# Ten value loads among the other loads, four-quadrant products, 4 KB output runs and hand-placed PSUM slots in a fused attention and token-mixing kernel

## The chip, the cores and the metric

One core of a Trainium2 chip. The metric is the device time of one execution in microseconds (us); most kernels ran 4 to 20 times, always beside the kernel before on the same chip. An execution counts as slow when it is over 1.5% above the fastest of its kernel; verdicts use the fast ones. A profile's span is about 2 us shorter than the time of its execution. Engines: PE is TensorE's products, PEld its weight loads, DVE is VectorE, ACT is ScalarE, POOL is GpSimd, SP issues the DMAs.

## The reference

Eight batches, eight heads, 576 tokens, head size 64. Attention in two parts, then a token-mixing MLP on x (576 x 512 per batch):

```python
q_d, k_d, v_d = (t.reshape(B, H, S // 4, 4, D).mean(axis=3) for t in (q, k, v))
out_up    = np.repeat(sm_attn(q_d, k_d, v_d), 4, axis=2)        # coarse
out_local = softmax(where(abs(i - j) < 4, q @ k.T / 8, -1e9)) @ v  # local band
x   = (out_up + out_local), heads side by side
w   = (x @ w_q) @ (x @ w_k).T / 8                                # per batch
out = maximum(w @ x, 0) @ w_out
```

## The kernel before

All loads and stores go through one DMA queue, issued by SP in program order. Per batch it loads q and k (1 MB each, runs of 1 KB), their last 64 tokens (`r`, runs of 256 B), and the value as ten pieces of 64 partitions (runs of 256 B):

```python
    def load_qk(b):
        q32 = big.tile([128, H, 4 * D], FP32, name="q32", tag="q32")   # two buffers each
        k32 = big.tile([128, H, 4 * D], FP32, name="k32", tag="k32")
        ...
        for src, t in ((q[b], q32), (k[b], k32)):
            sp.dma_start(t, _ap(src, 0, [[4 * D, 128], [S * D, H], [1, 4 * D]]))
        ...                                                             # r32 right behind
    def load_v(b):
        for n in range(NW):
            for c in range(2):
                sp.dma_start(v32[64 * c:64 * c + 64, n], ...)
```

The steps of several batches are interleaved by one list (the number is the batch relative to the iteration); a store is issued in the step that makes its rows:

```python
    ORDER = [
        (-2, "og1"), (-1, "wtd"), (0, "sums"), (1, "cast_qk"), (-1, "wt"), (0, "vd"), (0, "mask0"),
        (0, "score0"), (-1, "wks"), (2, "load_qk"), (1, "cast_v"), ...
        (2, "load_v"), (-1, "og0"), (0, "ca1"), (1, "tk"), (1, "tr"), (-1, "ol"), (0, "xt0"), ...
    ]
    def og(i):
        ...
        evac("og%d" % i, os_, p_)                                       # ACT, three buffers os
        sp.dma_start(out[b, 256 * i:256 * i + 256].rearrange("(m p) d -> p m d", p=128), os_)
```

Names used below, in the order of a batch: `psc` masks and local scores, `pcs` coarse scores, `pv` pooled value, `pav` local attention times value, `pca` coarse attention times value, `pw` and `pws`/`pwk` the projections, `pm` the product that `M` comes from, `pmx` the mixed rows (`rmx` after the relu), `po` and `pol` the last product.

The softmax here doesn't subtract the row's maximum and nothing guards it: scores larger than these inputs give would overflow.

## Time and profile before

| | before |
|---|---|
| time, median of 3 runs | 192.36 us (191.82 to 193.6) |
| one batch, start of `pw` to start of the next | 19.30 us |
| PE busy of these | 18.52 us |
| last value load landed | 151.5 us |
| clock granted to PE, mean | 0.95 |

### The profile page before, as it was taken

Reading aid. Unit: us, or ns where it says so; the run is one execution under the profiler, and the core shown is the slowest. Engines: PE = TensorE matmul, PEld = TensorE weight load, DVE = VectorE, ACT = ScalarE, POOL = GpSimd, SP = SyncE. Lnnn points to the kernel's source line nnn. Section 1 sums busy time; section 2 is a strip of 40 time slices with the busy share of each in tenths; the row PEclk is TensorE's granted clock in tenths of the full one; section 3 lists DMA queues with packets and bytes.
Section 4 is the critical chain, followed back from the end, with each engine's and each line's share of the span. In section 5 each row is a group of like instructions: output and inputs, shape, how many; then the busy total and the mean of one; then the engine's idle time right before and its main releaser. Section 6 shows DMA issues by size and latency. Waiting matters only on the chain.

```text
span 192.7 us, 6374 instructions
## 1 busy us (share of the span) xinstructions
PE 155.5 (81%) x2720; PEld 104.0 (54%) x2720; DVE 114.8 (60%) x286; ACT 110.7 (57%) x140; POOL 107.7 (56%) x122
## 2 busy tenths in 40 slices
PE   0034448885899989998999899989998999898790
PEld 0034227853576647664776476647764776465330
DVE  6263978754646566656665666566656665685220
ACT  2037134954565767576757675767576757633422
POOL 5701991099748991895479547954895476000000
PEclk9999555999789999999999999999999999999997
DMA  5999999899899799967999899969996943004215
GB/s 175 314 187 215 348 290 162 191 354 175 175 319 218 174 264 294 263 137 201 278 323 156 184 280 346 187 154 296 330 215 154 300 146 112 3 3 153 93 57 188
DMA packets 74027, 40.54 MB, mean 210 GB/s; under 512 B 52432, under 2 KB 68880, under 8 KB 74000
## 3 DMA queue, kind: packets, MB, share of 16 engines
q1 hardware_dynamic: 73920, 40.12, 81.7%
q8 instruction: 21, 0.34, 0.7%
q14 instruction: 6, 0.05, 0.1%
q10 hardware_dynamic: 80, 0.03, 0.1%
HBM read 30.67 MB, written 9.44 MB: 208 GB/s over the span
## 4 chain that ended last, share of the span: by engine, by line
PE 68%; DVE 17%; ACT 7%; issue 4%; POOL 2%; ACTq 0%; DVEq 0%
PE po L27 15%; PE psc L27 6%; PE pav L27 5%; PE pw L27 4%; PE px L27 4%; PE pca L27 4%; PE pol L27 4%; DVE kd_127 L27 3%; PE pv L27 2%; PE pcs L27 2%; ACT kT L27 2%; PE pod L27 2%; DVE rz L27 1%; PE pws L27 1%; PE pwd L27 1%
## 5 line engine op out<-in xcount | busy, mean ns | idle before, releaser
L27 ACT COPY os<-po 128x1024 f32<-128x1024 f32 x16 | 16.2, 1012 | 14.7 <-issue 8.3
L27 DVE RECIPROCAL rz<-pav 128x8 f32<-128x8 f32 x40 | 8.1, 204 | 13.4 <-PE pav L27 13.4
L27 PE MATMUL po<-wo_91,rmx_227 128*128 128x512 f16 x64 | 15.3, 379 | 0.6 <-ACT rmx_227 L27 0.6
L27 PE MATMUL po<-wo_91,rmx_212 128*128 128x512 f16 x64 | 15.1, 379 | 0.0
L27 DVE COPY xT<-px 128x928 f16<-128x928 f16 (+1 forms) x32 | 13.8, 451 | 0.6
L27 PE MATMUL pq_236<-id_67,q_229 128*128 128x128 f16 x16 | 1.9, 312 | 12.6 <-DVE q_229 L27 12.6
L27 PE MATMUL psc<-id_67,neg 64*128 64x232 f16 (+1 forms) x80 | 9.4, 278 | 2.8 <-DVE vblk_201 L27 2.8
L27 PEld LDWEIGHTS <-rmx_227 128*128 128x128 f16 x80 | 7.2, 98 | 8.1 <-ACT rmx_227 L27 0.7
L27 PE MATMUL psc<-qT,kT 64*64 64x58 f16 (+1 forms) x640 | 11.4, 198 | 0.0
L27 PEld LDWEIGHTS <-rmx_212 128*128 128x128 f16 x80 | 7.2, 98 | 6.6
L27 DVE RECIPROCAL rc<-pca 128x8 f32<-128x8 f32 (+1 forms) x16 | 3.4, 211 | 11.8 <-PE pca L27 11.8
L27 PEld LDWEIGHTS <-wqk_90 128*128 128x128 f16 x96 | 8.3, 98 | 3.7 <-issue 0.9
L27 PEld LDWEIGHTS <-kT 64*64 64x64 f16 x640 | 8.7, 113 | 2.1 <-issue 2.1
L27 ACT COPY odT<-pod 128x448 f16<-128x448 f16 (+1 forms) x16 | 5.6, 402 | 6.3 <-PE pod L27 6.3
L27 PE MATMUL pw<-xT,wqk_90 128*128 128x288 f16 x64 | 9.2, 286 | 0.0
L27 PEld LDWEIGHTS <-q_229 128*128 128x128 f16 x16 | 1.6, 146 | 12.6 <-DVE q_229 L27 12.6
L27 POOL CAST v_0_147<-v_79 128x2560 f16<-128x2560 f32 x1 | 3.1, 3129 | 9.3 <-DMA w_92<-in_moe_w_k_dram 9.3
L27 DVE TENSOR_TENSOR wT_219<-pw,wTd 128x576 f16<-128x576 f32 x4 | 3.0, 758 | 8.6 <-ACT wTd L27 8.6
L27 DVE COPY ol<-pol 64x512 f32<-64x512 f32 x8 | 5.5, 682 | 4.3 <-PE pol L27 4.3
L27 DVE TENSOR_TENSOR wT_204<-pw,wTd 128x576 f16<-128x576 f32 x4 | 3.0, 758 | 8.0 <-ACT wTd L27 6.6
L27 DVE TENSOR_SCALAR rmx_227<-pmx 128x1024 f16<-128x1024 f32 x4 | 4.9, 1224 | 4.1 <-PE pmx L27 4.1
L27 POOL CAST v_1_149<-v_255 128x2560 f16<-128x2560 f32 x1 | 2.3, 2323 | 8.6 <-DMA v_255<-in_v_dram 8.6
(542 smaller groups left out, 540.9 us busy)
## 6 DMA issues: line engine op xcount, KB each, us to landing
out_dram<-os SPq DMA_DIRECT2D x16, 512.0 KB, 4.4
v_79<-in_v_dram SPq DMA_DIRECT2D x10, 128.0 KB, 4.6
v_255<-in_v_dram SPq DMA_DIRECT2D x10, 128.0 KB, 5.4
v_583<-in_v_dram SPq DMA_DIRECT2D x10, 128.0 KB, 3.5
v_1024<-in_v_dram SPq DMA_DIRECT2D x10, 128.0 KB, 4.4
v_1497<-in_v_dram SPq DMA_DIRECT2D x10, 128.0 KB, 3.6
v_1970<-in_v_dram SPq DMA_DIRECT2D x10, 128.0 KB, 4.3
v_2443<-in_v_dram SPq DMA_DIRECT2D x10, 128.0 KB, 3.4
```

The source lines that it names most:

```text
L27: return lambda *a, **k: self._tc.keep_in_program_order(f_(*a, **k))
```

## The change

Its intent: shorten TensorE's work (four tiles at once in `pav`, two column tiles at once in `pm`, one `pol` for two batches), relieve POOL and DVE, start earlier, write longer runs, and spread the ten slow value loads between the fast loads of q and k. The core of the diff:

```diff
-    ps2 = ctx.enter_context(tc.tile_pool(name="ps2", bufs=3, ...))
-    ps1 = ctx.enter_context(tc.tile_pool(name="ps1", bufs=2, ...))
+    free = {2: [0, 1, 2], 1: [3, 4]}          # a slot is taken when it is free, can be held
...
-    def load_qk(b): ...                       # q32, k32: 2 + 2 buffers
+    def load_q(i): ...                        # q or k; tag="in32", bufs=3 for both
+    def load_r(b): ...
+    def load_v(n): ...                        # one of five pairs of pieces
...
-            pool.tensor_copy(v16[:, :, :, 0:64], v32)
+            evac("va" ..., v16[:, :, 0:4, 0:64], v32[:, :, 0:4])                    # POOL
+            for c in range(2):                                                       # ACT, DVE
+                evac("vb%d" % c ..., v16[64 - 64 * c:128 - 64 * c, :, 4:8, 0:64],
+                     v32[64 * c:64 * c + 64, :, 4:8])
...
-                                tile_position=(64 * c, 64 * c))                      # pav
+                                tile_position=(o, 64 * c))                           # o = 64 * (c ^ s_)
...
-            evac("M2", M2[0:64], p_[0:64], scale=s_mix)
+                pe.matmul(p_[64 * c:64 * c + 64], w_, x_, ..., tile_position=(0, 64 * c))
+            act.copy(half, p_[64:128])
+            dve.tensor_tensor(M2[0:64], p_[0:64], half, op=ALU.add)
...
-                        pe.matmul(p_[:, ff, :], rmx[:, r * S + c:r * S + c + 128], ...)
-                sp.dma_start(out[...].rearrange("(m p) d -> p m d", p=128), os_)
+                        pe.matmul(p_[:, ff, :], _ap(rmx, 512 * r + 2 * i + ff, [..., [4, 128]]), ...)
+        def so(i):                             # the store is a step of its own, placed by ORDER
+            return lambda: sp.dma_start(_ap(out[b], 2 * i * DM, [[4 * DM, 128], [1, 2 * DM]]), ...)
...
+    FIRST = [ ... ]                            # the start and batches 0 to 4 by hand
+    ORDER = [
+        (3, "load_r"), (0, "wtd"), (0, "wt"), (-1, "og1"), (1, "vd"), (1, "mask0"), ...
+        (2, "cast_r"), (2, "load_k"), (1, "score1"), ... (2, "load_v0"), ... (3, "load_v2"), ...
+        (2, "load_v3"), (2, "load_v1"), ... (-2, "so1"), (0, "ol"), ... (-1, "sol"),
+        (2, "load_v4"), ... (0, "og0"), ... (3, "load_q"), (2, "cast_v"), (-1, "so0"), (2, "tk"),
+    ]
```

In the last lines, q and k of a batch are no longer next to each other in the queue; both stores of a batch are issued about a period after their rows are made; and q and k share three buffers. The cast of `r` goes from POOL to ACT.

## The prediction

> **What bounds the kernel now.** I read the page first (busy times, the 40 slices, the queues), then the chain that ended last, then a table of windows cut at the end of each batch's `pwd`, then the issues on the DMA queue in order of time. The chain says that TensorE sets the end; in its steady part one batch takes 19.30 us (start of `pw` to start of the next `pw`), on the chain almost only PE pieces:
>
> ```profile
> 81.83 0.98 PE pw L27 x8
> ...
> 85.46 0.37 PE pav L27 x16
> 85.83 1.62 PE pm_1793 L27 x7
> ...
> 96.72 0.86 PE pol L27 x4
> ...
> 101.13 0.98 PE pw L27 x8
> ```
>
> The windows agree: PE is busy 18.52 of 19.30 us, at the full clock. The columns behind the length are PE, weight loads, DVE, ACT, POOL, then clock, DMA share, GB/s:
>
> ```profile
> 81.83:101.13 19.30, 18.52 (x342) 12.43 (x341) 12.32 (x29) 13.17 (x18) 13.58 (x13) 1.00 0.87 235
> 159.03:176.31 17.28, 16.50 (x306) 10.41 (x305) 11.73 (x27) 9.49 (x16) 3.25 (x6) 1.00 0.20 71
> 176.31:192.70 16.39, 9.21 (x62) 4.06 (x59) 3.18 (x5) 5.20 (x8) 0.00 (x0) 0.93 0.29 104
> ```
>
> But there is a second limit nearly as tight. The page's slices show the DMA engines at nine tenths or more until three quarters of the run, and the queue's issues form one unbroken stream up to 150 us:
>
> ```profile
> DMA  5999999899899799967999899969996943004215
> GB/s 175 314 187 215 348 290 162 191 354 175 175 319 218 174 264 294 263 137 201 278 323 156 184 280 346 187 154 296 330 215 154 300 146 112 3 3 153 93 57 188
> DMA packets 74027, 40.54 MB, mean 210 GB/s; under 512 B 52432, under 2 KB 68880, under 8 KB 74000
> ...
> 88.94 0.57 SPq L27 DMA_DIRECT2D out_dram<-os  x1
> ...
> 98.62 10.27 SPq L27 DMA_DIRECT2D v_1970<-in_v_dram  x10
> 108.99 1.13 SPq L27 DMA_DIRECT2D out_dram<-os  x1
> ...
> 129.28 0.57 SPq L27 DMA_DIRECT2D out_dram<-os  x1
> ```
>
> From store to store this stream takes 20.05 and 20.29 us, longer than PE's 19.30. The rate swings between about 150 GB/s (value loads, packets of 256 B) and 350 (q and k, 1 KB). PE is not starved only because the loads start two batches ahead. The lead shrinks, and the last value load is the proof:
>
> ```profile
> 151.85 2.32 POOL L27 CAST v_1_149<-v_2916 128x2560 f16<-128x2560 f32 x1 [4.56 <-DMA v_2916<-in_v_dram]
> 159.94 0.40 PE L27 MATMUL pv<-v_1_149,P_153 128*32 128x512 f16 x1
> ```
>
> The last batch's value lands at 151.8, its cast ends at 154.2, its first product starts at 159.94. Only 5.8 us of slack are left, however fast the engines become.
>
> Third, the start. In the chain, DVE's `sum`, `kd` and `kdt` hold everything from 18.22 to 27.2 us, and q waits behind constant fills on DVE until 11.4.
>
> **What the Trainium skill says.** "TensorEngine Tiling (Array Packing)", section Tiling Modes, Key Properties: different tiles can run at once, and changing the tiling mode drains the engine. The trace agrees on the first: scores, which use four 64x64 tiles, start 32 products in 0.26 us, eight ns apart; `pav`, which uses two tiles, starts 16 in 0.25, sixteen apart. After the four 32-column `pv` products the next mode starts 0.33 us later, against 0.215 between full products of that width. "DMA: Bandwidth & Descriptors", section Why small descriptors are slow, says a 256 B descriptor pays a fixed overhead of about a quarter; here value loads do run at under half of q's rate, so the trace agrees in direction, with more loss. The same page, Specifications, gives line rate from 512 B up: for the stores, 2 KB already, it promises nothing for 4 KB. "GPSIMD Engine Reference", Specifications, says its SBUF interface is shared with VectorE when VectorE has two SBUF inputs; the trace fits: `kd` took 1487 ns on DVE for batch 0 (POOL was casting) and 383 on POOL later.
>
> **The change, part by part, per batch.**
> - `pav`: four tiles in turn, and the value of the upper heads lies in the other half. From sixteen to eight ns a product: 16 x 8 ns = 0.13 us x 5 = -0.65 us of PE.
> - `pm`: 7 full products of 0.216 us become column-tiled pairs, four rounds: -0.65 us, and about 0.1 back for mode changes. But the sum of the two halves now takes an ACT copy of 64x512 (0.59, as `M` had) and a DVE add (0.69, as `x`) in series: some 0.7 us longer on the path in the tail, where nothing hides it.
> - `pol`: the last 64 rows of two batches share one product: -0.86 in every second batch, -0.43 on average.
> - masks and `vd` are split (9 more products a batch, same columns): +0.15.
> - In the chain, 87.84 to 89.79 is PE waiting in turn for DVE to empty `pav`, because the slots rotate. A new order with slots taken as they come free may win half: -0.7 (estimate).
> - Sum -2.2: PE's period becomes about 17.1 us.
> - ACT gets the second `rmx` (1.02), half of the upper value cast (64x1280 at the k cast's 1898 ns per 2048: 1.2), the remainder cast (0.6) and copies (0.7), `half` (0.6), half of `ol` (0.3), and gives up `vd`, `wTd`, `wd`, `M`, `mxr` (2.1): 13.2 + 2.3 = 15.5 us. DVE goes 12.3 to about 12.8, POOL 13.6 to about 11.5. All fit below 17.
> - Stores: `os` in 128 runs of 4 KB instead of 256 of 2 KB. The weights of the product are then read at a stride of four; `pws` already loads such strided weights at under 40 ns a product, and `po` has 216 ns to hide it. Worth nothing by itself, perhaps 0.2 us a batch of DMA.
> - Start: k and q come in halves, k first; sums of batch 0 move to PE (36 products) and ACT; constants are filled later. `pav` of batch 0 needs the value, which cannot land before about 18.5 us with the same stream, so its 28.3 becomes about 21: -7 us.
>
> **If PE alone decided:** `pw` of batch 0 at 40.0 - 7 = 33; next at +21 (22.5 before) = 54; five periods of 17.1 and a last one 2 us shorter (it has no next batch's transposes, as before: 17.28 against 19.30) = 154.6; tail 16.4 + 0.7 for `half` + 1 for both `rmx` now in series on ACT - 0.7 (`pm`) = 17.4. End: 172 us.
>
> **If the loads decide.** The bytes in front of the last load stay: 30.67 MB read, and in both programs eight `os` and four `ol` stores stand before it on the queue. So the landing stays near 151.8, less what a better mixture gives. Value loads are the stretch at low rate; ten of them placed between q, k and stores may run while large packets drain. I give it 4 us (estimate; half a us a batch of the 20). Landing 148; cast in three parallel parts, 1.3: 149.3. From `pv` of the last batch to the end took 192.7 - 159.94 = 32.8; less the PE savings of that stage and the tail (0.65 + 0.55 x 2 + 0.7 for the waits, 0.4 for `pol`), plus 1.7 in the tail: 31.6, and without the waits of a full engine, say 30. End: 179 to 181.
>
> The larger one rules, but the mixture may give more than 4 us, so I choose **178 us**.
>
> **The rivals.**
> 1. PE period rules (172). For it: PE is 96% busy, and the loads get spread on purpose. Against it: 20.05 us of queue time per batch that no part of the change takes away.
> 2. Loads rule fully, mixture gives nothing: 183 to 185. For it: all packets remain 256 B. Against: half-idle slices (6, 6, 4) show that the value stretches do not fill the engines.
> 3. Less prefetch starves PE: q and k now share three buffers where they had four, and a value is loaded, cast and used within about an iteration less than before; ACT at 15.5 with waits between could also become the pace: 186 to 191. For: stores wait for ACT, casts for loads, loads for casts. Against: casts of the batch before always precede the loads that need their buffer in program order by half an iteration.
> 4. Column tiles do not overlap in `pm` or `pav`: +1.3 a batch on PE, 18.4, still below the queue's 20. It would cost little.
>
> **Range and chances.** 172 is the floor that PE sets, 185 is rival 2: I take 171 to 186 for eight in ten. 2% faster means below 188.5, which only rival 3 in full would miss: faster 0.93, same 0.06, slower 0.01.
>
> **What would show it.** Right: the wait before the last cast of `v` still on DMA, landing at 146 to 150, and `pv` of the last batch within 2 us of that cast; PE pieces separated by waits on casts of q, k or v in the steady part; period 17.5 to 19; DMA share at nine tenths to the end of loading; `pm` four rounds at about 0.9 us, `pav` 16 at about 0.15; first `pav` near 21. Wrong: if the last load lands before 143, the queue was not at its limit and rival 1 holds; if ACT is busy over 95% in the steady windows, or queue issues wait on POOL casts for long, rival 3 does; if value stretches run over 200 GB/s, the mixture was worth more than I gave it.

## More of the kernel before

The chain, the windows, the DMA slices and the issues are shown in the prediction. Two more rows of the page matter later: busy tenths of PE and the granted clock, in 40 slices of 4.8 us.

```profile
PE   0034448885899989998999899989998999898790
...
PEclk9999555999789999999999999999999999999997
```

After the start PE is full and its clock stays full.

## The result, and the profile after

The changed kernel took **198.25 us** (median of 4: 197.92 to 201.45, the last one slow), beside 192.77 for the kernel before in the same rounds. The ratio is 1.028, 95% interval 1.021 to 1.035: slower by nearly 3%. A ratio here is the mean time of one kernel's fast runs over that of the other's fast runs of the same rounds, so it is not quite the ratio of the medians quoted.

The same two rows of the page, and the DMA row:

```profile
PE   0639495788799399995998998699895999999690
...
PEclk9999858599999859998899999969997999999997
DMA  5999998999879999989599889997799972202225
```

PE now has holes in the middle of the run (the 3, 5, 6, 5), and the clock falls after each of them. The DMA engines are full to the end of loading, as before. Cut at each start of `pw` (columns as in the prediction: length, PE, weight loads, DVE, ACT, POOL, clock, DMA share, GB/s):

```profile
59.51:81.03 21.52, 18.01 (x348) 12.62 (x346) 12.72 (x32) 14.05 (x19) 13.82 (x10) 0.84 1.08 242
...
101.38:120.98 19.60, 17.92 (x352) 12.14 (x350) 13.47 (x33) 15.13 (x20) 9.24 (x8) 1.00 0.95 238
120.98:142.46 21.48, 18.46 (x348) 12.63 (x346) 12.50 (x31) 14.77 (x19) 11.76 (x8) 0.92 0.91 218
...
163.59:179.23 15.64, 14.86 (x312) 9.87 (x310) 13.23 (x31) 11.35 (x14) 4.50 (x4) 1.00 0.15 58
179.23:196.00 16.77, 10.47 (x72) 5.00 (x69) 3.35 (x9) 6.04 (x7) 0.00 (x0) 0.93 0.36 138
```

The five steady periods take 20.8 us on average, where 17.1 were predicted, and no engine is full in them. What PE waits for has several names. The first kind is a pause inside one group of products, with nothing to wait for (the bracket is the idle time before, and its cause):

```profile
64.80 0.25 PE L27 MATMUL psc_1434<-qT,kT 64*64 64x56 f16 x7
...
68.46 0.32 PE L27 MATMUL psc_1434<-qT,kT 64*64 64x56 f16 x9 [3.42 <-issue]
```

In the middle of sixteen equal products TensorE stands still for 3.4 us. The trace's DMA records have one 16,384 B packet of the instruction queue at 65.4 us that took 1.4; there are 22 such packets, and PE with its weight loads has 5,624 instructions, about 256 to a packet. I read this as TensorE waiting for its own next instructions, a fetch; experiment 2 tests it. The second kind is a store:

```profile
126.03 1.01 ACT L27 COPY os<-po_2675 128x1024 f32<-128x1024 f32 x1 [2.46 <-DMA out_dram<-os]
...
127.10 0.38 PE L27 MATMUL psc_2749<-id_64,neg 64*128 64x232 f16 x4 [1.51 <-ACT os L27]
```

ACT cannot empty `po` into an output buffer whose last store has not landed, and PE waits for the slot of `po`. The page of waits counts (total us, times, longest):

```profile
ACT os L27 <- DMA out_dram<-os: 9.2, 5, 2.9
...
PE psc_1434 L27 <- issue: 3.4, 1, 3.4
```

Two smaller pauses, 0.49 at 119 and 0.89 at 140 us before `pk`, are of the second kind too. Between 60 and 160 us half clock set in within 3.3 us of the beginning of each pause of 1.5 us or more:

```profile
67.30:74.20 6.90, 5.74 (x91) 3.59 (x91) 2.83 (x8) 4.20 (x7) 1.89 (x1) 0.51 0.97 263
74.20:91.20 17.00, 14.94 (x293) 10.51 (x292) 11.42 (x25) 13.26 (x17) 11.58 (x8) 1.00 1.06 243
91.20:94.70 3.50, 3.35 (x52) 1.82 (x55) 2.17 (x5) 1.46 (x2) 0.00 (x0) 0.51 0.66 116
```

The Trainium skill, "TensorE: Matmul & The Clock Gate", Part 1, gives the idle state half the clock and a window of about 3.4 us after which a busy array is granted the full one. The trace agrees with the length: the half-clock stretches last 3.4 or 6.8 us. It does not agree that a whole idle window is needed: a pause of 1.51 us at 125.6 was followed by half clock from 128.8 to 132.2. Counted over all 20 traces, the clock changes lie on a grid of 3.41 us. Of the 711 grid windows at full clock after 45 us, half clock followed all 40 in which PE stood idle for 45% or more, 4 of the 22 between 36 and 45%, and none of the 649 below. So it is the idle share of a grid window that counts, and not the length of one pause: the 1.51 us and another 0.46 lie in one window and leave it idle for 57%. Between 60 and 160 us there are 17.1 us at half clock here (none before), which cost PE up to half of that.

The end, with first and last start in us:

```profile
L27 PE MATMUL pv<-v_1_100,P4rep x2: 276/281/286, 166.7 to 166.9; 128*128 128x256 f16 x2
L27 POOL CAST v_1_100<-v_2855 x1: 1262/1262/1262, 158.8 to 158.8; 128x1280 f16<-128x1280 f32 x1
L27 ACT CAST v_1_100<-v_2855 x1: 1263/1263/1263, 162.8 to 162.8; 64x1280 f16<-64x1280 f32 x1
L27 DVE CAST v_1_100<-v_2855 x1: 1886/1886/1886, 163.6 to 163.6; 64x1280 f16<-64x1280 f32 x1
```

The last value landed at 158.1 (151.5 before; 148 predicted), its three casts ended at 165.5, the first `pv` began at 166.4, and the program ended 29.6 us later. "Landed" is here and below the end of the last load packet; what waits for it sees it 0.2 to 0.8 us later. Did PE wait for this value?

```profile
149.10:184.00 34.90, 33.74 (x627) 22.55 (x626) 25.05 (x60) 24.12 (x31) 13.74 (x11) 0.95 0.46 131
```

```profile
166.39 0.29 PE L27 MATMUL pv<-v_1_100,P_102 128*32 128x256 f16 x1
```

It did not. PE was busy for 33.74 of the 34.90 us around the landing, and no idle time stands in a bracket behind its first `pv`.

What became slower is on the DMA engines. Both kernels load the same 66,560 packets: 16,384 of 1 KB and 50,176 of 256 B. Summed over the trace's records and divided by 16 engines, they take **124.1 us before and 136.5 us after**: a 1 KB packet 52.1 and 58.0 ns, a 256 B packet 22.6 and 24.6. The stores became cheaper, 31.8 and 27.9 us. I call the first number the load time of a kernel; it is the measure that the experiments follow. It has two weaknesses. The packets' records overlap (the DMA share of the period from 59.51 above is 1.08), so a longer record is not as much more work. And each kernel has one profile: kernels that differ only in small products of PE differ by 0.6 to 3.0 us (after_fix and after_stream_so with and without `pad64` in the table below).

### The profile page after: what moved, and what is told of

Its sections match the earlier page's. It is cut to its first block, busy times and chain, and to the rows that moved or that the text cites.

```text
span 196.0 us, 6577 instructions
## 1 busy us (share of the span) xinstructions
PE 156.8 (80%) x2812; PEld 107.5 (55%) x2812; DVE 114.8 (59%) x300; ACT 129.2 (66%) x160; POOL 94.0 (48%) x112
## 5 line engine op out<-in xcount | busy, mean ns | idle before, releaser
L27 PEld LDWEIGHTS <-kT 64*64 64x64 f16 x640 | 8.0, 119 | 7.3 <-issue 5.7
L27 PEld LDWEIGHTS <-rmx_98 128*128 128x128 f16 x64 | 7.0, 114 | 5.6 <-ACT rmx_98 L27 0.4
L27 PEld LDWEIGHTS <-rmx_86 128*128 128x128 f16 x64 | 6.9, 113 | 5.0
L27 PEld LDWEIGHTS <-neg 64*128 64x128 f16 x112 | 4.3, 99 | 9.8 <-issue 9.4
L27 PEld LDWEIGHTS <-wqk_69 128*128 128x128 f16 x96 | 8.0, 98 | 2.1 <-issue 0.6
L27 PEld LDWEIGHTS <-k_163 128*128 128x128 f16 x32 | 3.3, 144 | 6.4 <-ACT k_163 L27 6.4
L27 PE MATMUL pk_173<-id_64,k_163 128*128 128x128 f16 x8 | 1.0, 310 | 5.7 <-POOL P_106 L27 5.7
L27 POOL CAST v_0_99<-v_2373 128x1280 f16<-128x1280 f32 x1 | 1.7, 1707 | 7.6 <-DMA v_2373<-in_v_dram 7.6
L27 POOL CAST k_2096<-k_1801 128x2048 f16<-128x2048 f32 x1 | 1.9, 1898 | 6.2 <-PE pav_2026 L27 6.2
L27 POOL CAST q_917<-q_856 128x2048 f16<-128x2048 f32 x1 | 1.9, 1890 | 6.1 <-DMA q_856<-in_q_dram 6.1
L27 DVE TENSOR_SCALAR wk_95<-pwk,rows 128x256 f16<-128x256 f16 (+1 forms) x8 | 2.0, 296 | 4.6 <-PE pwk L27 4.6
L27 POOL CAST v_2_101<-v_1898 128x1280 f16<-128x1280 f32 x1 | 1.7, 1701 | 6.2 <-DMA v_1898<-in_v_dram 6.2
L27 DVE CAST vd_0_80<-pv 128x512 f16<-128x512 f32 x4 | 2.8, 693 | 3.2 <-PE pv L27 3.2
L27 PEld LDWEIGHTS <-q_169 128*128 128x128 f16 x32 | 3.2, 141 | 2.5 <-DVE one_109 L27 1.4
L27 DVE CAST vd_1_92<-pv 128x512 f16<-128x512 f32 x4 | 2.8, 694 | 3.0 <-PE pv L27 2.8
L27 PE MATMUL pol<-wo_70,rest 128*128 128x512 f16 x16 | 4.4, 399 | 0.1
L27 ACT COPY qT<-pr 128x256 f16<-128x256 f16 x8 | 2.9, 368 | 2.1 <-PE pr L27 2.1
L27 POOL CAST k_1625<-k_1225 128x2048 f16<-128x2048 f32 x1 | 1.9, 1897 | 5.1 <-DMA k_1225<-in_k_dram 5.1
L27 PEld LDWEIGHTS <-M_0_84 128*128 128x128 f16 x32 | 2.5, 109 | 3.0 <-issue 1.4
L27 POOL CAST q_538<-q_509 128x2048 f16<-128x2048 f32 x1 | 1.9, 1895 | 4.6 <-DMA q_509<-in_q_dram 4.6
```

The costliest lines, as they stand in the source:

```text
L27: return lambda *a, **k: self._tc.keep_in_program_order(f_(*a, **k))
```

## The experiments

All runs together. "Load time" is the sum just described; a star marks a profile that fell on a slow run, so that its two numbers on the right are only indications.

| run | median us (runs) | ratio of fast runs to before | load time | last value landed |
|---|---|---|---|---|
| before | 192.77 (4) | 1 | 124.1 | 151.5 |
| after | 198.25 (4) | 1.028 | 136.5 | 158.1 |
| after_nov | 182.66 (4) | 0.945 | fewer loads | |
| before_nov | 200.94 (4) | 1.040 | fewer loads | |
| after_so | 198.76 (4) | 1.020 | 130.6 | 156.8 |
| after_pad64 | 195.76 (20) | 1.001 | 134.2* | 160.4* |
| after_pad128 | 200.22 (4) | 1.021 | 134.6 | 158.9 |
| after_2kb | 196.73 (20) | 1.005 | 133.9* | 158.2* |
| after_block | 198.09 (4) | 1.013 | 137.0* | 159.2* |
| after_oldorder | 223.05 (4) | 1.156 | 128.8 | 163.5 |
| after_buf4 | 198.01 (4) | 1.021 | 138.6* | 159.0* |
| after_qk2 | 195.24 (20) | 1.004 | 130.2 | 149.5 |
| after_stream | 200.77 (4) | 1.032 | 125.8 | 147.2 |
| before_mix | 196.18 (9) | 1.007 | 133.7 | 144.7 |
| after_fix | 195.02 (15) | 0.997 | 130.3* | 152.6* |
| after_fix_pad64 | 193.16 (17) | 0.989 | 130.9 | 154.0 |
| after_stream_so | **188.84** (4) | **0.975** | 129.7 | 148.2 |
| after_stream_so_pad64 | 190.41 (4) | 0.984 | 126.7 | 148.6 |
| after_stream_so2 | 194.26 (4) | none given | 128.4* | 154.6* |
| after_stream_so_apart | 195.91 (4) | 1.011 | 133.4 | 148.2 |

Where a kernel ran 15 or 20 times, its times spread over 6 to 9 us without gaps, and the ratio of its fast runs flatters it; there I go by the median.

**1. Is it the value traffic?** No value loads from batch 2 on, the two buffers used again. Its output is wrong, which doesn't matter for the time.

```diff
         def f_(b):
+            if b >= 2:
+                st[b]["v32"] = st[b % 2]["v32"]
+                return
```

> The changed kernel, but the value is loaded for the first two batches only and used again for the rest (wrong result on purpose). Theory Q (the load stream sets the end of the changed kernel): the time falls to the end that the prediction worked out for TensorE alone, 171 to 177 us, with a period near 17.2. Theory E (the new order couples the engines: ACT, stores, PSUM slots wait for one another): it stays above 190 us.

Measured: 182.66 us, a fall of 16 us (interval of the ratio 0.939 to 0.950).

```profile
77.00:94.00 17.00, 16.60 (x348) 11.78 (x346) 13.67 (x31) 14.73 (x19) 11.46 (x8) 1.00 0.76 236
94.00:111.70 17.70, 17.33 (x353) 12.17 (x351) 13.85 (x32) 15.31 (x20) 11.54 (x9) 1.00 0.61 189
```

PE is full and its period is 17.0 to 17.7, but for one of 18.6: the arithmetic does what was planned for it. What makes 20.8 of it is the traffic. The floor is higher than I had expected, 180.5 us of span instead of 172. The longer period has a fetch pause of its own, with the DMA engines almost idle (share 0.03 in these 1.36 us):

```profile
118.75 0.28 PE L27 MATMUL pav<-v,E 64*64 64x65 f16 x9 [1.36 <-issue]
```

So a fetch can stop PE without a full queue; the pauses of 3.4 us and more stand only in kernels with all loads.

The same edit in the kernel before:

> The kernel before with the same loads taken away (wrong result on purpose). Theory Q: before was still bound by TensorE, so its period stays at 19.3 and the time at 188 to 193 us. If loads already bound it somewhere, it falls below 186.

Measured: 200.94, slower. The profile shows periods of 19.3 to 20.0, but for one of 22.2 with a pause of 2.09 us inside `pav` and half a clock behind it. So the kernel before is not bound by its loads. Why it lost more than these 2.9 us is open.

**2. One kind of wait at a time.** First the stores: issued a quarter into the next period, and in the period of their evacuation.

```diff
-        ... (-2, "so1") ... (-1, "so0"), (2, "tk")
+        ... (1, "score1"), (-1, "so0"), ... (1, "av2"), (-1, "so1"), ...
```

> The changed kernel with the two stores of a batch issued earlier in the order: the first a quarter into the next period (it was at its end), the second in the same period as its evacuation (it was one period later). Arithmetic and buffers are the same. Theory W (ACT waits for an output buffer whose store was issued late, PE's slot for the next scores waits for ACT, and each pause over 1.5 us is followed by 3.4 us of half clock): the 9.2 us of ACT waiting for stores fall below 3, PE's pauses of 0.59, 1.51 and 2.00 us before masks go, with one or two half-clock stretches: 191 to 194 us. Rival (the waits only take up slack that a late input or an instruction fetch would take up otherwise): the pauses go, others come in their place, within 1 per cent of 198.

Measured: 198.76. The 9.2 us of ACT waiting for stores are gone from the page of waits; in their place stand these:

```profile
PE pav L27 <- issue: 4.1, 2, 3.6
PE psc L27 <- issue: 4.1, 1, 4.1
```

The fetch pauses grew from 3.42 and 1.98 to 4.08 and 3.62, and two pauses before and inside `pcs` appeared, 1.42 for `kd` and 1.88 for no wait that the profile shows. The load time fell to 130.6, though no load was moved. Then the fetches, moved by small products at the start, where TensorE waits for the first key anyway:

```diff
+    def pad():
+        for _ in range(2):
+            p_ = psm(name="ppad")
+            for _ in range(16):                 # 32 for after_pad128
+                pe.matmul(p_[:, 0:16], id16, id16[:, 0:16], start=True, stop=True)
...
+        (0, "pad"), (0, "load_k"), ...
```

> The changed kernel with 32 tiny matmuls (64 instructions) at the very start, where TensorE waits for the first key anyway. They move every later boundary of the 256-instruction blocks that TensorE fetches by 64 instructions. Theory F (pauses of 3.42 at 65 us and 1.98 at 89 us are TensorE waiting for a block of instructions; where the boundary falls in dense scores or pav the fetch comes too late): the start is unchanged within 0.5 us, the two pauses move to other groups or vanish, and the time changes by more than 1 per cent either way, 192 to 201. Rival (the pauses are something of these groups themselves): pauses at the same groups, time within 0.5 per cent of 198.

> The same with 64 tiny matmuls (128 instructions): half a block. Theory F: pauses at yet other groups than in the changed kernel and in the run with 64; time 192 to 201. Rival: pauses at the same groups, time within 0.5 per cent of 198.

Measured: 195.76 and 200.22. Between 60 and 160 us the run with 128 has no pause inside a group over 1 us left, and the run with 64 has one, of 1.41 inside `po` at 96, where the changed kernel had none: the fetch pauses do hang on where a block ends. The store pauses grew instead. In the run with 128:

```profile
ACT os L27 <- DMA out_dram<-os: 10.9, 3, 5.1
```

and PE's pauses before masks are 4.27, 1.00 and 2.87 us (0.59, 1.51 and 2.00 after the change; the run with 64 shows the same picture, but its profile fell on a slow run). So taking away one kind of wait lengthens another; each alone is worth about one per cent or nothing. What they share is the queue.

**3. The shape of the stores.** Contiguous weights and runs of 2 KB, as before.

```diff
-  pe.matmul(p_[:, ff, :], _ap(rmx, 512 * r + 2 * i + ff, [[row(rmx), 128], [4, 128]]), ...)
+  pe.matmul(p_[:, ff, :], rmx[:, r, 128 * (2 * i + ff):128 * (2 * i + ff) + 128], ...)
```

> The changed kernel with the outputs as before: contiguous weights for the last product, 256 runs of 2 KB a store instead of 128 of 4 KB. If runs of 4 KB harm (the records show 164 ns a packet of 4 KB against 99 for 2 KB of before; a packet of a load has to wait behind a longer one), it gets faster by 1 to 3 per cent (192 to 196). If they help as intended, it gets slower by up to 1.5 per cent (199 to 201). If they do nothing, as I predicted blind: within 0.7 per cent of 198, and the product po keeps its time per matmul.

Measured: 196.73 over 20 runs, between 193.5 and 200.6. It covers the 198.25 of the changed kernel with its 4 runs; a gain of up to one per cent can be neither shown nor ruled out. The load time is 133.9 in a slow run's profile, too near to 136.5 to say that the runs of 4 KB slow the loads.

**4. The order of the loads.** First, the ten value loads of a batch in one block, but q and k still apart:

```diff
-  (2, "load_k"), ... (2, "load_v0"), ... (3, "load_v2"), ... (2, "load_v3"), (2, "load_v1"), ...
+  (2, "load_k"), (2, "load_v0"), (2, "load_v1"), (2, "load_v2"), (2, "load_v3"), (2, "load_v4"), ...
```

> The changed kernel with the ten value loads of a batch in one block again, behind q and k, nothing else moved. Theory M (mixing value loads with q, k and stores makes the queue slower): the last value lands some 6 to 8 us sooner and the time falls to 188 to 193 us. Rival (the queue is as slow in either order, or the lead is the trouble): 195 us or more.

Measured: 198.09; in the fast runs 1.3% above the kernel before, unclear. No quick gain. Next, the changed arithmetic in the whole order of before:

```diff
-    FIRST = [...by hand...]; ORDER = [...by hand...]
+    ORDER = [...of the kernel before; load_q, load_k, load_r and the five load_v in place of load_qk and load_v...]
```

> The arithmetic, engines and 4 KB stores of the changed kernel, with the order of steps, the loads and the number of input buffers of the kernel before. If the order of the change is at fault (any of its parts), this gives what the prediction expected of the arithmetic, 180 to 187 us. If the arithmetic or its engines are at fault (ACT at 15.5 us a batch, column tiles), it stays at 194 us or more.

Measured: 223.05. It stays far above 194, which by the expectation speaks against the arithmetic; after_nov has shown that the arithmetic can keep its pace. I think that the new `pm`, with `half` on ACT and the add on DVE, needs other work between it and `pmx`, which the old order does not give (1.72 us of pause there in every period). So this run cannot tell whether the new order is at fault. But its load time is 128.8. That gave the next pair: q, k and r back to back, in two buffers each,

```diff
-  tag="in32", bufs=3
+  tag="qk"[i] + "32"
-  (2, "load_k"), ... (3, "load_r") ... (3, "load_q")
+  (3, "load_q"), (3, "load_k"), (3, "load_r")
```

> The changed kernel with only q, k and remainder of a batch issued back to back (own buffers, two each); value loads stay spread as the change has them. Theory D in its narrow form (k next to q is what counts): 1 KB packets at 52 to 54 ns, time 188 to 193. Theory D in its wide form (any 256 B load near a 1 KB load slows it): 55 to 58 ns and 193 to 197. Rival P: 197 to 200.

and with the value loads in one block behind them as well, about two batches ahead, in the hand-placed start too (where the weights' loads moved up). This is the load stream of before:

```diff
+  (1, "mask1"), (3, "load_q"), (3, "load_k"), (3, "load_r"), ...
+  (1, "ca0"), (3, "load_v0"), (3, "load_v1"), (3, "load_v2"), (3, "load_v3"), (3, "load_v4"), ...
```

> The changed kernel's arithmetic, engines, store steps and order of compute, with the load stream of the kernel before: q, k and the remainder of a batch back to back, then its ten value loads in one block, about two batches ahead, in separate buffers for q and k (two each). Theory D (the queue is full from the first microsecond in both kernels; in the changed one the same packets take longer, 58.7 ns instead of 52.1 for 1 KB up to 145 us, about 6 us of the queue in all, because q and k are issued among 256 B loads and not next to each other): 1 KB packets come back to 52 to 54 ns, the last value lands by 152, and the time is 183 to 190, below the kernel before. Rival P (pauses of TensorE for fetches, stores and casts cause the loss, the packets are only slower because of them): packets may change, the pauses remain, within 1.5 per cent of 198.

Measured: 195.24 and 200.77. The queue did what was expected: load times of 130.2 and 125.8, 1 KB packets at 53.4 and 53.2 ns, the last value at 149.5 and 147.2. The time did not follow in the second. Its profile shows why:

```profile
110.87 1.01 ACT L27 COPY os<-po 128x1024 f32<-128x1024 f32 x1 [12.33 <-DMA out_dram<-os]
...
111.93 0.57 PE L27 MATMUL psc<-id,neg 64*128 64x232 f16 x4 [11.16 <-ACT os L27]
```

With loads two batches ahead, a store that is issued late stands behind a whole block of them. One wait of 11 us eats the gain; the periods before it took 17.2 and 17.3 us. (In after_qk2 a pause of 5.37 at 49 us is ACT waiting for `r` of batch 2, which I had put behind q and k.)

The opposite, in the kernel before: value loads put between q and k.

```diff
-  sp.dma_start(q32, ...); sp.dma_start(k32, ...); r32
+  sp.dma_start(q32, ...); value pairs 0 and 1; sp.dma_start(k32, ...); value pair 2; r32
```

> The kernel before with its loads mixed from batch 2 on: q, four value loads, k, two value loads, remainder at the place of the q and k loads, the other four value loads at the place of the value loads. Everything else as it was. Theory D: 1 KB packets go from 52.1 to 55 to 58 ns, the last value lands 2 to 6 us later and the time rises to 195 to 199. Rival (mixing is harmless or useful, as I thought blind): 1 KB packets stay at 52, landing at 150 to 152, time 191 to 194.

Measured: 196.18, in the fast runs 0.7% slower (interval 1.003 to 1.012). The load time rose from 124.1 to 133.7, so the order lengthens the packets' records in this kernel too. For the rest neither theory got it right: the 256 B packets became slower (22.6 to 25.2 ns), the 1 KB ones hardly (53.4), and the last value landed at 144.7, earlier than before, with some value loads now issued earlier. So a longer load time does not by itself mean a later landing. In the profile PE's period stayed 19.3: this kernel has room for it.

**5. Only the buffers.** In all runs that mended the order, q and k also had two buffers each. Alone:

```diff
-  tag="in32", bufs=3
+  tag="qk"[i] + "32"
```

> The changed kernel with two buffers each for q and k in place of three shared ones; order and everything else the same. If the shared buffers slow the loads: the load packets take 128 to 131 us of an engine in all (136.5 in the changed kernel), 1 KB packets at 53 to 54 ns, and the time is 190 to 195. If it is the order of the loads alone: 134 to 138 us, 1 KB packets at 56 to 59 ns, time within 1.5 per cent of 198.

Measured: 198.01, load time 138.6 (in a slow run's profile). The buffers alone are not it.

**6. Both together.** q and k back to back and early stores, the value loads left spread; and the same with 64 small instructions:

```diff
+  kernels of 2 (after_so) and 4 (after_qk2, with r left where the change has it) in one
```

> The changed kernel with q and k of a batch issued back to back in their own buffers (remainder and value loads where the change has them) and the stores issued earlier. If slow packets (a) and late stores (b) are the loss: 1 KB packets at 53 to 54 ns, last value landing at 148 to 152, no wait of ACT for a store over 1 us, and 182 to 188 us. If either only hides another wait of the same size: 192 to 197.

> after_fix with 64 small instructions of TensorE at its start, which moves the boundaries of the instruction blocks. Instruction fetches (c) should show as pauses at other groups than in after_fix or not at all; time within 2 per cent of after_fix, either way. If no pause over 1.5 us is left between 60 and 160 us: 180 to 185.

Measured: 195.02 and 193.16, above the 182 to 188 that I had expected if these two were all. There was still a pause of 4.64 at 82 us in the second, before masks, in which ACT waited for `r`; and the last value landed at 154.0, not before 152.

The load stream of before and early stores:

```diff
+  after_stream with (1, "score1"), (-1, "so0"), ... (1, "av2"), (-1, "so1"), ...
```

> The run with the load stream of before (200.8 us, one wait of 11.2 us for a store at 100.8) with the stores issued earlier. If that wait was the late store: it goes, and the time falls by 8 to 13 us to 188 to 192, since periods without a wait took 17.3 us there. If the wait is the full queue itself, whatever is issued when: another wait of 5 us or more stands in its place, 195 to 201.

Measured: **188.84** (187.99 to 189.74), ratio 0.975 with interval 0.971 to 0.979. It beats both kernels. The page's row of the clock, and two of its periods:

```profile
PEclk9999955557999999999999999999999999999996
```

```profile
62.20:79.00 16.80, 15.83 (x348) 11.56 (x346) 13.17 (x32) 13.84 (x19) 11.01 (x8) 1.00 0.89 220
...
96.60:117.00 20.40, 17.46 (x352) 12.06 (x350) 13.81 (x31) 15.15 (x20) 11.53 (x9) 1.00 1.07 276
```

After the start there is no half clock until the tail. The longer period still holds a 2.54 us pause for a store; the grid of the clock cuts it into two windows that are idle for 31 and 43%. Four kernels now make a square of two edits: neither 198.25, early stores alone 198.76, load stream alone 200.77, both 188.84. So it takes both; beside the kernel before on the same chips the ratios are 1.028, 1.020, 1.032 and 0.975. The load edit is a bundle, though: order, place in time, buffers and the start. Is the result luck with the instruction blocks?

> after_stream_so with 64 small TensorE instructions at the start. If 188.8 does not hang on where the instruction blocks end: 187 to 191. If it was luck with the blocks: pauses of 1.5 us or more inside groups of products appear, 192 to 196.

Measured: 190.41 (189.74 to 191.85), ratio 0.984, interval 0.977 to 0.992, on another chip. Not luck, though two store pauses of 2.51 and 3.23 are left. I tried to remove the first by placing that store in front of the loads:

```diff
-  (1, "mask1"), (3, "load_q"), (3, "load_k"), (3, "load_r"), ... (1, "score1"), (-1, "so0")
+  (1, "mask1"), (-1, "so0"), (3, "load_q"), (3, "load_k"), (3, "load_r"), ... (1, "score1")
```

> after_stream_so with the first store of a batch moved in front of the q, k and remainder loads in the queue (it stood behind them). The 2.54 us pause of TensorE at 101 us shrinks below 1 us and the time falls by 1 to 4 us, to 185 to 188. If the pause is not due to the place of this store: pause and 188.8 stay.

Measured: 194.26, from 190.0 to 196.44. A miss: ACT's waits for stores went, and pauses of 3.18, 1.81 and 3.60 us stand elsewhere (in a slow run's profile). They are ACT's waits for the last 64 tokens `r`, whose cast the change had moved to ACT and whose load now stands behind a store:

```profile
ACT r L27 <- DMA r<-in_k_dram: 15.3, 5, 6.8
```

So the gain of after_stream_so is real but not robust against small moves. Last, only the distance of q and k:

```diff
-  (3, "load_q"), (3, "load_k"), (3, "load_r"), ... (3, "load_v0"), (3, "load_v1"), (3, "load_v2"), ...
+  (3, "load_q"), (3, "load_v0"), (3, "load_v1"), (3, "load_v2"), (3, "load_k"), (3, "load_r"), ...
```

> after_stream_so with only this undone: for batches 2 and 4 to 7 six value loads stand between q and k, as in the changed kernel other loads stood there; everything else, buffers and stores too, is the same. If the distance of q and k slows packets and this costs time: 1 KB packets between 40 and 145 us at 56 to 60 ns (53.3 in after_stream_so), last value load landing 3 to 7 us later than 148.2 and 192 to 197 us. If the distance does nothing by itself: 53 to 54 ns, landing within 1.5 us, time within 1 per cent of 188.8.

Measured: 195.91 (194.62 to 199.12), in the range expected, and the load time rises from 129.7 to 133.4. But my picture of it was wrong: the 1 KB packets stay at 53.6 ns, the 256 B ones go from 24.0 to 25.0, and the last value lands at 148.2 as before. PE pauses by 3.73, 1.81 and 2.25 us at 51, 74 and 96. The first is ACT waiting for `r`, which the edit pushed back together with k; the other two are fetches. That the edit costs time is shown; that it does so through slower q and k packets is not, and 3.7 us of load time are hardly more than the 3.0 between after_stream_so and its version with 64 small instructions.

The queue's own row (packets, MB, share of 16 engines' span) sums it up, for before, after and after_stream_so in turn:

```profile
q1 hardware_dynamic: 73920, 40.12, 81.7%
```

```profile
q1 hardware_dynamic: 71904, 40.12, 84.8%
```

```profile
q1 hardware_dynamic: 71904, 40.12, 85.3%
```

By the spans of 192.7, 196.0 and 187.6 us these are 157.4, 166.2 and 160.0 us of all 16 engines: the records of the same bytes sum to 8.8 us more after the change (by the records, loads +12.4 and stores -3.9), and 2.6 more in the version that wins.

## Why the prediction was wrong

Right were most sizes on TensorE. `pav` starts its 16 products in 0.13 us. `pm` goes in pairs, though its tail chain (PE pauses 1.39 us for `half` and the add) is as long as feared. The period without value traffic is 17.0 to 17.7, once 18.6, against the 17.1 predicted. ACT's 14.1 to 15.4 us a period lie just under the 15.5, and did not become the pace. The tail from `pw` took 16.8 (17.4 predicted), and 29.6 us went from the last `pv` to the end (30 predicted). For `pol`, the masks and the 4 KB runs no run showed a need of correction.

Wrong was the step **"The larger one rules"**. It takes the end as the later of two sums that do not touch, PE's and "If the loads decide", so that a full queue can cost time only through its last landing. It cost time in every period. PE's own sum goes from the predicted 172 to the 196.0 of the profile like this: `pw` of batch 1 began at 59.5 and not at 54, +5.5; five periods took 20.8 and not 17.1, +18.6; the last one 15.6 and not 15.1, +0.5; the tail -0.6. Of the 18.6, 2.6 are there without value traffic (88.1 us for five periods in after_nov), and 16.0 come with it. Of the five periods' 104.1 us, PE's pauses from 65 to 149 us are 11.3 (5.9 inside groups, read as fetches, and 5.5 for stores; after_nov has 2.2 of the first kind), and the 17.1 us at half clock are up to 8.5 more (an estimate: half of it). Together they cover the difference of 16.0, with 1.7 to spare.

The sum of the loads was wrong as well, but it did not decide. **"Landing 148"** came out at 158.1, 10.1 later: the clause **"the landing stays near 151.8, less what a better mixture gives ... I give it 4 us"** failed, for the mixture gave nothing and the load time rose by 12.4 us. The term **"cast in three parallel parts, 1.3"** took 7.4, 6.1 more, since ACT and DVE came to their parts only 4.7 and 5.5 us after the landing. With 0.9 until `pv` and 0.4 less to the end, 179.3 becomes 196.0 on this way too. But PE did not wait for the value, as shown above, and an early landing does not bring the end forward: the last value landed at 147.2 in after_stream, 149.5 in after_qk2 and 148.2 in after_stream_so_apart, as predicted, and these took 200.77, 195.24 and 195.91. That `pv` came within 2 us of the last cast, a sign set for "right", was chance.

Wrong, and part of the 5.5: **"its 28.3 becomes about 21: -7 us"** at the start. The first `pav` came at 23.9, and `pw` of batches 0 and 1 began at 42.2 and 59.5, not 33 and 54, and without value traffic at 43.5 and 60.0. With 3 us more in the periods this lifts the floor from 172 to the 180.5 of after_nov. Even with a perfect queue the prediction would have been too low by a little. One line was misread, too: of the half-idle slices held against rival 2, the 4 (154 to 159 us) lies behind the last value load, at 151.5.

Rival 3 came nearest, and I gave it almost no weight. I had listed "stores wait for ACT, casts for loads, loads for casts". Missing were ACT waiting for stores, instruction fetches, and the half clock behind the pauses.

The test that I had set, DMA at nine tenths to the end of loading, came true and could not tell the cases apart: a full queue says nothing of how long the same packets take.

Shown, then: the traffic costs the changed kernel 16 us; PE loses them in pauses and half clock all along the run; late stores make such pauses when the loads stand in front of them (after_stream against after_stream_so, where only the stores moved, 12 us); and of the square, only both edits together gain, 2.5% against the kernel before. Argued, not shown: that the pauses trade places because the queue's time is what is short, and that longer packet records make it short. The load time does follow the order of the loads (126 to 131 with q and k together, 133 to 139 with them apart), but it fell to 130.6 in after_so, where only stores moved, and it foretells neither the landing (133.7 and 144.7 in before_mix) nor the time (125.8 and 200.77 in after_stream). Untested is a rival: which engine waits. Between 45 and 165 us only POOL waits for DMAs in the kernel before. The change put the cast of `r` and part of the value's on ACT, whose copies PE needs, and stored late what ACT has to overwrite; in 14 of the 16 profiles of changed kernels with all loads, all but after_so and after_oldorder, ACT waits for a store or for `r` in these microseconds, 3.5 us or more in all. No run put the cast of `r` back on POOL. Open: why a packet takes longer in that order (1 KB packets that start in a microsecond with over nine tenths of the engines' time take 51.1 ns before and 57.4 after), which order is best, and why before_nov loses 4%.

## What to carry to other kernels

Do not add a full DMA queue to a plan as one landing at the end: look for every engine that waits for a transfer and that the busiest engine needs, here ACT for stores and for `r`. Issue a store as soon as its rows are there, since behind a full queue its landing is what holds the output buffer, and keep loads of one kind together until a run shows otherwise. And if a removed wait does not move the time, see which wait has grown: single removals gave about one per cent or nothing here, the load stream of before and early stores together about 5% against the changed kernel by the medians.

## What the Trainium skill lacked or had wrong

- "Runtime: NRT & Kernel Launch", Instruction fetch mechanics, has the refill of instructions in blocks of 256 over a DMA queue, and calls its cost mostly hidden. These traces show 22 packets of 16,384 B on the instruction queue during the run, about one per 256 instructions of TensorE, and pauses of PE that go with them, up to 4.1 us in fast runs, and one of 1.36 us even with the DMA engines almost idle.
- "DMA: Bandwidth & Descriptors", Why small descriptors are slow, prices a descriptor by its size. Here the records of the same 66,560 load packets sum to 124.1 us of an engine before and 136.5 after the change, and to 130.6 when only two stores a batch are moved; I found no page that prices a packet by its neighbours on the queue.
- "TensorE: Matmul & The Clock Gate", Part 1, asks in its table of states for an idle window of about 3.4 us for the half clock. (Further down it tells of a kernel whose short idles were enough, without a share.) In these traces half clock followed all 40 windows of 3.41 us that were idle for 45% or more, and none of the 649 that were idle for under 36%.
